# A planner counts eight transfers in flight on each queue: attention and a two-layer network on one core

## The chip, the cores and the metric

One core of a Trainium2 chip runs the whole program in one launch. The metric is the device time of one execution in microseconds (us), taken as the median over runs. TensorE (PE in the views) multiplies matrices, VectorE (DVE), ScalarE (ACT) and GpSimd (POOL) do element work, SyncE (SP) issues most transfers.

## The reference

```python
def _attn_ref(q, k, v, f):                     # (8, 8, 576, 64) each, f (8, 8, 576)
    scores = scale * np.matmul(q, k.transpose(0, 1, 3, 2))
    cum = np.cumsum(np.log(np.clip(f, 0.0001, 1.0)), axis=-1)
    scores = np.where(causal, -1000000000.0, scores + cum[:, :, :, None] - cum[:, :, None, :])
    attn = softmax(scores)                     # max taken off, sum + 1e-9
    return np.matmul(attn, v)

def _moe_ref(x, w_in, w_out, alpha):           # x (4608, 512), w_in (512, 2048)
    h = x @ w_in
    g = np.maximum(h, 0.0) + alpha * np.minimum(h, 0.0)
    return g @ w_out
```

The attention's output, with batch and position as rows and the 8 heads of 64 side by side, is the x of the two-layer network. All is 32-bit.

## The kernel before

**Attention.** The 64 heads are taken as 32 pairs, four pairs (0 to 3) for each of 8 batches; pair n belongs to batch n // 4. Pairs 0 to 8 transpose their exponentials on TensorE. Pairs 9 to 31 go through the function `turned`: TensorE makes the scores of both heads in one step of 24 matmuls (`run1`) and the last 64 query rows in a step of 6 (`run2`); VectorE adds the decay and takes the maximum (line 853, and 917 for the tail), ScalarE takes exponentials (line 833), VectorE turns 32x32 blocks (line 890), and sixteen transfers of 100 KB put the blocks in place (line 927, `big<-big`), eight of them issued by SyncE and eight by GpSimd. The product with v (`pv`, 60 matmuls) of pair n stands on TensorE behind `run1` of pair n + 2. ScalarE copies it out (966, 967), GpSimd scales it (989, 992), ScalarE rounds it (995) and GpSimd takes what the rounding left (996): rounded value and remainder together are a split x, one of four column groups of its batch.

**First layer.** For each batch there are 16 column blocks of h (`ffn1`, block 0 to 15). A block is two halves of six matmuls of 128x512 on one bank: the first half needs x of the batch's first two pairs, the second half x of its last two. ScalarE and VectorE evict a bank (1042, 1044) into one of three slots of a ring (`hs`, a part of `hx`), and a transfer of 256 KB stores the slot to DRAM (1046, `hd<-hx`). A slot is free again when its store has landed. The buffers of split x are six, of which a batch needs four; those of the first two column groups come free when the first half of block 15 is through. First-layer blocks of one batch fill TensorE beside the attention of the next two.

**Second layer.** From about 603 us the stored h comes back and is multiplied in 18 units; nothing of the attention is left by then.

**What sets the order.** Every step is an `op` with an engine, an estimated length, a key and its inputs. `Plan.run` plays the program through once while it is built: at each turn it looks over the steps whose inputs are planned, gives each the earliest start `s` that its engine, inputs and buffers allow, takes the smallest `(s, key)` on each engine and emits the earliest of these. Each engine runs its instructions in that order. A store of h has key -1000 and so goes first among steps that can start at the same time. A transfer (`kb` above 0) keeps its queue for its issue alone, some 0.4 us, and is planned to land after a common channel has moved it:

```python
if o.kb:
    self.chan = max(self.chan, s + 1.4) + o.kb / (220.0 if s < FAR else 280.0)
    end = self.chan + (0.0 if s < 4 else 2.0)
```

The built program has a rule of its own, which can be read in its waits: SyncE's transfers use eight channels (DMAHW0 to DMAHW7) in turn, and each waits until the one before it on its channel, the eighth ahead of it, has landed. It does so before the change and after it. The planner before does not know of it.

Of the kernel before, what the change touches and what calls it, by code (L numbers as in the profile page):

```python
# [53 lines left out]
class Store:  # L54


    def __init__(self, items):
        self.items, self.rings = items, []
        self.free = [(0.0, i) for i in range(len(items))]
# [30 lines left out]

SLACK = {"DVE": 1.12, "ACT": 1.08, "POOL": 1.05}
ENGS = ("PE", "ACT", "DVE", "POOL", "SP", "-")


class Plan:
    def __init__(self):
        self.now = dict.fromkeys(ENGS, 0.0)
        self.chan = 0.0
        self.ops = []
        self.banks = self.fill = None  # L100
        self.rnd = random.Random(SEED)
# [27 lines left out]
    def run(self):  # L129
        ops, self.ops = self.ops, []  # L130
        cand = {e: [] for e in ENGS}
        for o in ops:
            if o.n == 0:
                cand[o.eng].append(o)
        left = len(ops)
        mine = set(ops)
        while left:
            best = None
            for e in ENGS:
                t0 = self.now[e]  # L140
                pick = None
                for o in cand[e]:
                    r = o.ready
                    for b in o.bufs:
                        if b.t is not None:
                            continue
                        k = b.seq - b.ring.next
                        if k and not any(o2.ring is b.ring and o2.seq == b.ring.next for o2 in o.bufs):
                            r = None
                            break  # L150
                        a = b.ring.at(k)
                        if a is None:
                            r = None
                            break
                        if a > r:
                            r = a
                    if r is None:
                        continue
                    s = t0 if t0 > r else r
                    if pick is None or (s, o.key) < pick[:2]:  # L160
                        pick = (s, o.key, o)
                if pick is not None and (best is None or pick[0] < best[0]):
                    best = pick
            assert best is not None, "the plan is stuck"
            s, _, o = best
            self.t = s
            cand[o.eng].remove(o)
            left -= 1
            end = s + o.ns
            t0_, new = self.now[o.eng], []  # L170
            if o.two:
                end += max(0.0, self.now["POOL"] - s)
            self.now[o.eng] = end
            if o.kb:
                self.chan = max(self.chan, s + 1.4) + o.kb / (220.0 if s < FAR else 280.0)
                end = self.chan + (0.0 if s < 4 else 2.0)
            o.start, o.end = s, end
            for b in o.bufs:
                if b.t is not None:
                    continue  # L180
                st = b.ring.store
                f = min(st.free)
                st.free.remove(f)
                b.i, b.t = f[1], st.items[f[1]]
                if o.eng == "PE" and st is self.banks:
                    new.append((f[0], b.t))
                b.ring.next += 1
                b.ring.held += 1
            if new and self.fill and s < FILL:
                self.fill(new[0][1], s - max(t0_, new[0][0]))  # L190
            o.fn()
            for b in o.bufs:
                b.left -= 1
                b.last = max(b.last, end)
                if b.left == 0:
                    b.ring.held -= 1
                    b.ring.store.free.append((b.last + 0.3, b.i))
            for c in o.outs:
                c.n -= 1
                c.ready = max(c.ready, end + self.lag(o, c))  # L200
                if c.n == 0 and c in mine:
                    cand[c.eng].append(c)
# [1210 lines left out]
```

## Time and profile before

| | |
|---|---|
| median of 3 runs | 1011.52 us (1011.07 to 1012.36) |
| profiled execution | 1009.73 us, of which the span from first to last instruction is 1007.9 us |
| TensorE | busy 998.3 us (99%), mean granted clock 0.998 |
| VectorE, ScalarE, GpSimd | 815.2 us (81%), 592.7 us (59%), 394.4 us (39%) |
| transfers | 191.05 MB, 190 GB/s in the mean |

A group of matmuls in the timeline is given with its start and length; since matmuls are pipelined, the next group starts some 0.1 us before such a length is over. A wait in square brackets is idle time of the engine and what ended it. All matmuls stand on the helper's line 371, so they are told apart by what they read: `xx,wi` is the first layer, `Qhl` the scores, `big,vr` the product with v.

### The profile page before, as it was taken

The numbers are of one execution on the slowest core, as the hardware profiler recorded it, in microseconds if no ns is written. First come the engines' busy times: TensorE is split into PE (matmuls) and PEld (weight loads), VectorE is DVE, ScalarE is ACT, GpSimd is POOL, SyncE is SP. The second block draws the span as 40 slices with busy tenths as digits, with TensorE's granted clock in tenths as the row PEclk, the third lists the DMA queues.
The fourth block names the chain that finished last, engine by engine and source line by source line (L and its number), as shares of the span: only waits on it lengthen the run. The fifth ranks groups of instructions, "written<-read, shape, count | busy, mean of one in ns | idle before, by whom it ended". The sixth has DMA issues, their size and how long they took to land.

```text
span 1007.9 us, 21097 instructions
## 1 busy us (share of the span) xinstructions
PE 998.3 (99%) x7492; PEld 867.6 (86%) x7492; DVE 815.2 (81%) x1597; ACT 592.7 (59%) x1297; POOL 394.4 (39%) x635
## 2 busy tenths in 40 slices
PE   9999999999999999999999999999999999999998
PEld 6778888888878878888888888899999999999998
DVE  7878768888768838858754988699999999999994
ACT  7987876766657637656543766564553636444541
POOL 4575758799978857869650100000000000000000
PEclk9999999999999999999999999999999999999999
DMA  7988748989997987978867677543434344334421
GB/s 221 262 243 240 233 128 216 250 260 252 262 244 207 254 220 214 255 228 230 221 186 234 208 221 215 162 128 116 146 127 140 112 148 146 121 112 160 131 85 42
DMA packets 167545, 191.05 MB, mean 190 GB/s; under 512 B 22089, under 2 KB 116593, under 8 KB 167441
## 3 DMA queue, kind: packets, MB, share of 16 engines
q1 hardware_dynamic: 161264, 170.66, 57.8%
q0 software_dynamic: 5888, 18.85, 7.1%
q8 instruction: 59, 0.97, 0.4%
q14 instruction: 46, 0.37, 0.1%
q10 hardware_dynamic: 288, 0.20, 0.1%
HBM read 102.74 MB, written 48.80 MB: 150 GB/s over the span
## 4 chain that ended last, share of the span: by engine, by line
PE 88%; DMA 8%; SPq 2%; DVE 1%; issue 1%; ACT 0%; DVEq 0%; ACTq 0%
PE bank L371 84%; DMA big<-big 3%; PE bank L591 3%; DMA hd<-hx 2%; SPq L927 1%; DMA vr<-in_vv_dram 1%; DMA rqk<-in_qk_dram 1%; DVE big L890 0%; PE bank L439 0%; DMA Z<-c 0%; DVE hx L1044 0%; ACT hx L1042 0%; PE bank L473 0%; DMA rd<-st 0%; DVE Z L498 0%
## 5 line engine op out<-in xcount | busy, mean ns | idle before, releaser
L371 PE MATMUL bank<-xx,wi 128*128 128x512 f32 x1728 | 409.0, 393 | 0.3 <-POOL xx L996 0.3
L371 PEld LDWEIGHTS bank<-xx,wi 128*128 128x128 f32 x1728 | 320.3, 188 | 67.3 <-POOL xx L996 0.9
L371 PE MATMUL bank<-wi,gh 128*128 128x256 f32 (+1 forms) x1308 | 183.0, 301 | 0.0
L371 PE MATMUL bank<-wot,gh 128*128 128x256 f32 (+1 forms) x1308 | 183.0, 301 | 0.0
L371 PEld LDWEIGHTS bank<-wot,gh 128*128 128x128 f32 x1308 | 171.9, 191 | 9.6
L371 PEld LDWEIGHTS bank<-wi,gh 128*128 128x128 f32 x1308 | 171.8, 191 | 9.5
L833 ACT ACTIVATE big<-big,st 128x384 f32<-128x384 f32 (+4 forms) x207 | 118.6, 575 | 40.6 <-DVE st L853 40.5
L1044 DVE SCALAR_TENSOR_TENSOR hx<-bank,sa,hx 128x512 f32<-128x512 f32 x96 | 71.3, 744 | 82.8 <-ACT hx L1042 81.2
L1042 ACT ACTIVATE hx<-bank,ab 128x512 f32<-128x512 f32 x96 | 66.0, 688 | 94.8 <-PE bank L371 66.3
L890 DVE STREAM_TRANSPOSE big<-big 128x1408 f32<-128x1408 f32 (+2 forms) x69 | 86.6, 1274 | 20.7 <-DMA vr<-in_vv_dram 9.7
L371 PEld LDWEIGHTS bank<-big,vr 128*64 128x64 f32 x1884 | 89.2, 137 | 12.3 <-issue 3.2
L371 PE MATMUL bank<-big,vr 128*64 128x128 f32 (+2 forms) x1884 | 95.8, 260 | 2.1 <-DVE st L616 1.1
L545 POOL TENSOR_TENSOR Qhl<-rqk,Qhl 128x640 fp32r<-128x640 f32 (+1 forms) x56 | 83.4, 1497 | 31.8 <-ACT Qhl L544 29.3
L927 POOL DMA_DIRECT2D big<-big x184 | 92.1, 507 | 8.5 <-DVE big L890 4.8
L371 PE MATMUL bank<-Qhl 64*128 64x512 f32 (+6 forms) x840 | 93.4, 326 | 1.5 <-DVE hx L1044 1.5
L371 PEld LDWEIGHTS bank<-Qhl 64*128 64x128 f32 (+1 forms) x840 | 74.9, 186 | 17.5 <-issue 8.8
L517 POOL TENSOR_TENSOR Z<-Z,hx 128x384 f32<-128x384 f32 x60 | 54.8, 924 | 27.0 <-DMA Z<-c 17.2
L1290 ACT ACTIVATE gh<-hg 128x768 fp32r<-128x768 f32 x28 | 23.7, 848 | 65.4 <-issue 28.4
L1290 ACT ACTIVATE gh<-wx 128x768 fp32r<-128x768 f32 x28 | 23.7, 847 | 63.5 <-PE bank L371 28.4
L1293 DVE TENSOR_TENSOR gh<-hg,gh 128x1792 fp32r<-128x1792 f32 x28 | 56.5, 2017 | 1.6 <-ACT gh L1292 1.6
L1293 DVE TENSOR_TENSOR gh<-wx,gh 128x1792 fp32r<-128x1792 f32 x28 | 56.2, 2017 | 0.1
L996 POOL TENSOR_TENSOR xx<-hx,xx 128x512 fp32r<-128x512 f32 x32 | 41.9, 1317 | 27.6 <-ACT xx L995 27.1
(157 smaller groups left out, 1315.3 us busy)
## 6 DMA issues: line engine op xcount, KB each, us to landing
hd<-hx SPq DMA_DIRECT2D x144, 256.0 KB, 3.7
big<-big SPq DMA_DIRECT2D x184, 100.0 KB, 5.4
big<-big POOLq DMA_DIRECT2D x184, 100.0 KB, 5.2
rqk<-in_qk_dram SPq DMA_DIRECT2D x28, 608.0 KB, 4.9
hg<-hd SPq DMA_DIRECT2D x28, 512.0 KB, 4.9
wx<-hd SPq DMA_DIRECT2D x28, 512.0 KB, 4.2
vr<-in_vv_dram SPq DMA_DIRECT2D x32, 320.0 KB, 3.7
big<-in_w_in_dram SPq DMA_DIRECT2D x16, 512.0 KB, 5.2
```

Source lines behind the costliest of these rows:

```text
L371: pe.matmul(o, lhsT, rhs, start=start, stop=stop)
L517: m1 = op("POOL", c_po(128 * 3), lambda z4=z4: po.tensor_tensor(z4()[:, 6:9], z4()[:, 0:3], tb(3), ALU.add), kc + 0.1, got + [o_mask], [bZ])
L545: o2 = op("POOL", c_po(w), lambda hi=hi, lo=lo, raw=raw: po.tensor_tensor(lo(), raw(), hi().bitcast(F32), ALU.subtract), kc, [o1], [bqk, bQ])
L591: pe.transpose(t[:, c : c + 128], src[:, 128 * j : 128 * j + 128], ident)
L833: sums.append(op("ACT", c_exp(w), lambda: ac.activation(at(), at(), AF.Exp, bias=lo()[:, col : col + 1], scale=-1.0, accum_out=su()[:, col ...
L890: ve.transpose(t_t[:, :, c0 : c0 + 32 * (b1 - b0)].rearrange("p k (b c) -> p k b c", c=32), bE.t[:, 128 * off : 128 * (off + b1 - b0)].rea ...
L927: moves.append(op(n_, 550 if i % 2 else 450, lambda a=a, k=k, q_=q_: q_.dma_start(bM.t[32 * k : 32 * k + 32, a], t_t[32 * a : 32 * a + 32, ...
L996: xl = op("POOL", c_po(512), lambda: po.tensor_tensor(bx.t[:, 1], bxs.t[:, 0:512], bx.t[:, 0].bitcast(F32), ALU.subtract), st, [xh], [bxs, ...
L1042: cp = op("ACT", c_act(512), lambda bh=bh, bs=bs, fc=fc: ac.activation(bs.t, bh.t, AF.Relu, scale=ab[:, fc : fc + 1]), -1000, [last, o_sg] ...
L1044: cp = op("DVE", c_dve(512), lambda bh=bh, bs=bs, fc=fc: ve.scalar_tensor_tensor(bs.t, bh.t, sa[:, fc : fc + 1], bs.t, ALU.mult, ALU.add), ...
L1290: h0 = op("ACT", c_acs(3 * 128 * GW), lambda bhx=bhx, bgh=bgh: ac.activation(bgh.t[:, 0, 0:3], bhx.t[:, 1:4], AF.Copy), key, o1, [bhx, bgh])
L1293: his, rdy = [h0, h1], [op("DVE", c_tt(7 * 128 * GW), lambda bhx=bhx, bgh=bgh: ve.tensor_tensor(bgh.t[:, 1], bhx.t[:, 1:8], bgh.t[:, 0].bi ...
```

## The change

The planner keeps, for each queue, the planned landings of its transfers; a transfer is not planned to start before the landing of the eighth one ahead of it on its queue. No step, length, key or seed changes; the same instructions are emitted in another order.

```diff
+DEEP = 8
@@ class Plan, __init__
         self.chan = 0.0
+        self.flying = {e: [] for e in ENGS}
@@ run
                     s = t0 if t0 > r else r
+                    if o.kb and len(self.flying[e]) >= DEEP:
+                        s = max(s, self.flying[e][-DEEP])
                     if pick is None or (s, o.key) < pick[:2]:
@@
                 end = self.chan + (0.0 if s < 4 else 2.0)
+                self.flying[o.eng].append(end)
```

Lines of the kernel after are five higher (371 becomes 376). TensorE's order is the same up to where the trace has 79 us and again from the product with v of the last pair (535 us). Between them `run1` of pairs 10 to 18 stands behind 36 to 60 more first-layer matmuls than before, of pairs 19 to 22 behind 36 more, and of the pairs from 23 on at nearly the old place (24 fewer to 6 more).

TensorE before, at the passage from batch 1 to batch 2 of the first layer (`big,vr`: product with v of pair 12; each `xx,wi ... x6` is one half of a block, each `x12` a block):

```order
L371 MATMUL bank_83<-xx,wi 128x512 x6
L371 MATMUL bank_76<-big,vr_105 64x128 x20
L371 MATMUL bank_79<-big,vr_105 64x64 x10
L371 MATMUL bank_78<-Qhl_99 128x320 x3
L371 MATMUL bank_81<-Qhl_99 128x256 x3
L371 MATMUL bank_83<-xx,wi 128x512 x6
L371 MATMUL bank_80<-xx,wi 128x512 x12
L371 MATMUL bank_82<-xx,wi 128x512 x12
```

TensorE after, the same passage (`big,vr_106`: product with v of pair 11; then `run2` of pair 13, block 15 of batch 1, four first halves and, from `bank_78` on its second row, the second halves of batch 2):

```order
L376 MATMUL bank_78<-big,vr_106 64x128 x20
L376 MATMUL bank_82<-big,vr_106 64x64 x10
L376 MATMUL bank_80<-Qhl_100 128x320 x3
L376 MATMUL bank_79<-Qhl_100 128x256 x3
L376 MATMUL bank_83<-xx,wi 128x512 x12
L376 MATMUL bank_78<-xx,wi 128x512 x6
L376 MATMUL bank_81<-xx,wi 128x512 x6
L376 MATMUL bank_77<-xx,wi 128x512 x6
L376 MATMUL bank_76<-xx,wi 128x512 x6
L376 MATMUL bank_78<-xx,wi 128x512 x6
L376 MATMUL bank_81<-xx,wi 128x512 x6
L376 MATMUL bank_77<-xx,wi 128x512 x6
```

Before, the second half of block 0 of batch 2 follows its first half at once, and between pair 11's product with v and that second half stand the scores and the product with v of pair 12. After, pair 12 is behind the passage, and 39 first-layer matmuls stand between pair 11's product with v and the first matmul that reads pair 11's x.

SyncE before, the load of q and k (`rqk`) of pair 21, which stands right ahead of the eight moves (`big<-big`) of pair 17, with the channel that each transfer waits for:

```order
L491 DMA rqk_98<-in_qk_dram 128x2x608 [waits DMAHW1_49,Pool_49]
L927 DMA big<-big 32x800 [waits DMAHW2_49,DVE_49]
L927 DMA big<-big 32x800 [waits DMAHW3_49]
L927 DMA big<-big 32x800 [waits DMAHW4_49]
L927 DMA big<-big 32x800 [waits DMAHW5_49]
L927 DMA big<-big 32x800 [waits DMAHW6_49]
L927 DMA big<-big 32x800 [waits DMAHW7_49]
L927 DMA big<-big 32x800 [waits DMAHW0_49]
L927 DMA big<-big 32x800 [waits DMAHW1_49]
L821 DMA vr_105<-in_vv_dram 128x640 [waits DMAHW2_49,PE_49]
L1046 DMA hd<-hx 128x4x128 [waits DMAHW3_49,DVE_49]
L1046 DMA hd<-hx 128x4x128 [waits DMAHW4_49,DVE_49]
```

SyncE after, the load of the same pair's q and k:

```order
L496 DMA rqk_98<-in_qk_dram 128x2x608 [waits DMAHW3_49,Pool_49]
L1051 DMA hd<-hx 128x4x128 [waits DVE_49]
L932 DMA big<-big 32x800 [waits DMAHW5_49,DVE_49]
L932 DMA big<-big 32x800 [waits DMAHW6_49]
L932 DMA big<-big 32x800 [waits DMAHW7_49]
L932 DMA big<-big 32x800 [waits DMAHW0_49]
L932 DMA big<-big 32x800 [waits DMAHW1_49]
L932 DMA big<-big 32x800 [waits DMAHW2_49]
L932 DMA big<-big 32x800 [waits DMAHW3_49]
L932 DMA big<-big 32x800 [waits DMAHW4_49]
L943 DMA rd_64<-st_110 128x32 [waits DMAHW5_49,DVE_49]
L826 DMA vr_105<-in_vv_dram 128x640 [waits DMAHW6_49,PE_49]
```

Before, the last of the eight moves waits for the channel of the load (DMAHW1), and the two next stores of h stand behind it. After, the moves are those of the same pair 17, one store has come between load and moves, the next stands behind all twelve, and now the seventh move waits for the load's channel (DMAHW3 there).

## Rows read from the trace of the kernel before

**Rows 1.** The page, part 1: busy time, share and instructions of each engine.

```profile
PE 998.3 (99%) x7492; PEld 867.6 (86%) x7492; DVE 815.2 (81%) x1597; ACT 592.7 (59%) x1297; POOL 394.4 (39%) x635
```

**Rows 2.** Busy time of each engine in four stretches (header: the columns).

```profile
core 0: us, PE busy (x) PEld busy (x) DVE busy (x) ACT busy (x) POOL busy (x), PEclk, DMA share, GB/s
80.00:280.00 200.00, 200.00 (x1679) 165.87 (x1678) 160.59 (x397) 139.82 (x375) 158.99 (x239) 1.00 0.82 228
280.00:320.00 40.00, 38.49 (x287) 31.66 (x286) 28.15 (x70) 24.31 (x64) 30.76 (x50) 0.96 0.86 234
360.00:380.00 20.00, 18.73 (x146) 15.46 (x145) 8.06 (x20) 9.14 (x19) 9.94 (x15) 1.00 0.82 226
380.00:1000.00 620.00, 620.00 (x4345) 558.94 (x4344) 520.52 (x836) 329.08 (x589) 117.34 (x188) 1.00 0.55 164
```

**Rows 3.** TensorE in order of time, 294 to 306 us (start, length, what, idle before).

```profile
294.76 0.97 PE L371 MATMUL bank<-Qhl 64*128 64x512 f32 x6
296.06 0.44 PE L371 MATMUL bank<-Qhl 64*128 64x384 f32 x1 [0.34 <-DVE hx L1044]
297.68 1.49 PE L371 MATMUL bank<-Qhl 64*128 64x384 f32 x17 [1.17 <-DVE hx L1044]
299.09 2.88 PE L371 MATMUL bank<-xx,wi 128*128 128x512 f32 x6
301.90 3.30 PE L371 MATMUL bank<-big,vr 128*64 128x128 f32 x60
305.13 1.06 PE L371 MATMUL bank<-Qhl 128*128 128x320 f32 x6
```

**Rows 4.** The same view, 364 to 379 us.

```profile
363.81 5.18 PE L371 MATMUL bank<-xx,wi 128*128 128x512 f32 x22
369.27 3.45 PE L371 MATMUL bank<-xx,wi 128*128 128x512 f32 x14 [0.28 <-POOL xx L996]
372.65 2.19 PE L371 MATMUL bank<-Qhl 64*128 64x512 f32 x24
375.84 2.98 PE L371 MATMUL bank<-big,vr 128*64 128x128 f32 x60 [0.99 <-DVE hx L1044]
```

**Rows 5.** The same view, 218 to 235 us.

```profile
218.05 2.98 PE L371 MATMUL bank<-big,vr 128*64 128x128 f32 x60
220.97 1.06 PE L371 MATMUL bank<-Qhl 128*128 128x320 f32 x6
221.87 6.99 PE L371 MATMUL bank<-xx,wi 128*128 128x512 f32 x30
228.79 2.19 PE L371 MATMUL bank<-Qhl 64*128 64x512 f32 x24
232.50 2.99 PE L371 MATMUL bank<-big,vr 128*64 128x128 f32 x60
```

**Rows 6.** ScalarE in order of time, two evictions of the first layer.

```profile
294.54 0.69 ACT L1042 ACTIVATE hx<-bank,ab 128x512 f32<-128x512 f32 x1 [7.14 <-DMA hd<-hx]
...
360.09 0.69 ACT L1042 ACTIVATE hx<-bank,ab 128x512 f32<-128x512 f32 x1 [6.27 <-DMA hd<-hx]
```

**Rows 7.** SyncE in order of time: transfers as it issued them.

```profile
278.42 0.46 SPq L491 DMA_DIRECT2D rqk<-in_qk_dram  x1
278.97 10.05 SPq L927 DMA_DIRECT2D big<-big  x8
...
290.24 0.92 SPq L1046 DMA_DIRECT2D hd<-hx  x2
```

**Rows 8.** SyncE's waits from 250 to 380 us: total, times, longest.

```profile
SPq L927 <- DMA rqk<-in_qk_dram: 8.7, 3, 4.0
```

**Rows 9.** Line 491 (the q and k loads): issue to landing, all 28.

```profile
DMA to landing us min/median/max: 4.3/4.9/10.1
```

**Rows 10.** GpSimd in order of time: low parts of x.

```profile
230.75 1.28 POOL L996 TENSOR_TENSOR xx<-hx,xx 128x512 fp32r<-128x512 f32 x1 [0.18 <-ACT xx L995]
245.67 1.30 POOL L996 TENSOR_TENSOR xx<-hx,xx 128x512 fp32r<-128x512 f32 x1
...
366.68 2.54 POOL L996 TENSOR_TENSOR xx<-hx,xx 128x512 fp32r<-128x512 f32 x2 [2.14 <-ACT xx L995]
```

## The prediction

> **What bounds the kernel now.** I read the page's table of engines first. TensorE is busy for 99% of the span [rows 1], so an edit of the order can only win what TensorE loses: idle time, and time at a lower clock. The other four engines count only where TensorE waits for them. The table of stretches says where it loses. From 80 to 280 us and from 380 to 1000 us it is busy all the time, and the granted clock is 1.00 [rows 2]. Between them it falls short: 1.51 us of idle time from 280 to 320 us, at a mean clock of 0.96, and 1.27 us from 360 to 380 us at 1.00 [rows 2]. The order after is the old one up to about 79 us and again from 535 us on, so these places are all that it can win. (The start, before 79 us, is left as it is.)
>
> TensorE in order of time shows what each costs, three places in all.
>
> At 294.8 us `run1` of pair 19 waits 0.34 and 1.17 us for banks that ScalarE's side of the eviction frees late (the waits end on DVE, L1044). Then it runs slow: six 128x512 first-layer matmuls take 2.88 us, where 30 take 6.99 us [rows 3, 5]. Taken start to start, the 24 score matmuls, the six and the 60 of `pv` take 305.13 − 294.76 = 10.37 us [rows 3]. Clean, the same take 2.19 + 6 × 0.2307 + 2.92 = 6.49 us: 2.19 is the length of 24 score matmuls in one piece, 2.92 is 220.97 − 218.05, and 0.2307 is (228.79 − 221.87) / 30 [rows 5]. So **3.9 us** are lost. Of these 1.7 are the clock's: (301.90 − 299.09) − 1.38 = 1.43 on the six and (305.13 − 301.90) − 2.92 = 0.31 on the 60. The six run at half the speed of rows 5, that is at 1.2 GHz for 2.4.
>
> At 369.27 us the second halves of a batch wait for x: 36 matmuls take 372.65 − 363.81 = 8.84 us, clean 36 × 0.2307 = 8.30, so **0.5 us** [rows 4]. At 375.84 us a `pv` waits 0.99 us, and its 60 matmuls then take their usual 2.98 us: **1.0 us**, no lower clock [rows 4]. In sum 3.9 + 0.5 + 1.0 = 5.4 us.
>
> ScalarE's rows name the cause: evictions of the first layer at 294.54 and 360.09 us had waited 7.14 and 6.27 us for a store of h to land, since all three slots were taken [rows 6]. SyncE's rows say why the store was late. A load of q and k goes out at 278.42, the eight moves behind it take 10.05 us to issue, and the two stores behind them come only at 290.24 [rows 7]. The eighth move needs the load's channel, and the load lands late: issue to landing is 4.9 us in the median and 10.1 at most [rows 9]. SyncE's waits from 250 to 380 us have this in three places, 8.7 us in all [rows 8].
>
> **The change, part by part.** It adds and removes no instruction, so every term is a wait.
>
> *Stores ahead of moves.* SyncE's order after has a store between that load and the moves, and the load's channel is wanted by the seventh move. One slot of three is then free before the moves begin. The next store stands behind moves, decay rows and v, as before. ScalarE had to wait some 7 us for three slots; one early store lets it go on by one bank of twelve matmuls, 12 × 0.2307 = 2.8 us. In addition 36 to 60 more first-layer matmuls now stand ahead of `run1` of pairs 10 to 22, 36 × 0.2307 = 8.3 us: `run1` wants its banks and its q and k later than before, while the moves still end when they ended. 2.8 + 8.3 = 11.1 us is more than the 7.14 [rows 6], so I take the wait of `run1` as gone, with the 0.99 at `pv`, which has the same cause, and the 0.5 at the second halves, which now stand elsewhere. Bounds: nothing won at all (0), or all 5.4. I take **−5.4**, the nearer to the rows, as the needed slack is covered with 4 us to spare.
>
> *Loads of w_in for the last blocks* go out later, behind stores, from 80 to 150 us. TensorE has no idle time there now [rows 2], and its first-layer backlog hides them. With that cover gone it is a wait like the 0.99 of rows 4; as for a gain, there is no idle time to win. I take 0.
>
> *The new passage from batch 1 to batch 2.* Here the order takes a cover away. The second half of a block of batch 2 reads pair 11's x. Before, pair 12's scores and its `pv` stood between pair 11's `pv` and that half. After, `run2` and 39 first-layer matmuls do: 0.90 us (221.87 − 220.97) + 39 × 0.2307 = 9.9 us [rows 5]. The path of x from `pv` to the last low part can be read on the neighbours: `pv` of pair 12 ends at 218.05 + 2.98 = 221.03 and the low part at 230.75 + 1.28 = 232.03, so 11.0 us; pair 13's `pv` ends at 232.50 + 2.99 = 235.49, its low part at 245.67 + 1.30 = 246.97, so 11.5 us [rows 5, 10]. TensorE then waits 1.1 to 1.6 us; I take **+1.3**. Bounds: nothing, where GpSimd and ScalarE meet less work on that path; and 7.14 us, where ScalarE, which must copy and round on it, stands in a wait like that of rows 6. I take a value near the low end, since it comes from two rows of the same step. A gain is excluded, as no idle time stands there [rows 2].
>
> *Its clock.* An idle time of 0.34 + 1.17 us was followed by the half clock, one of 0.99 us was not [rows 3, 4]. 1.3 lies nearer to 1.51 (0.2 off) than to 0.99 (0.3 off), so I add the clock's **+1.7**; the bounds are 0 and 1.7.
>
> The sum is −5.4 + 1.3 + 1.7 = −2.4 us. The profiled execution took 1009.73 us, the median of the runs is 1011.52, which is 1.79 more; I take the difference over to after. So a profiled execution of 1007.3 and a median of **1009.1 us**.
>
> **The rivals.**
>
> *The new passage is hidden as well.* Then 1011.52 − 5.4 = 1006.1. For it: 1.3 us is little, and rows 10 show that GpSimd's step itself waits only 0.18 us, so a quieter ScalarE would shorten the path. Against it: both neighbours agree within 0.5 us.
>
> *The landing of the load sets the pace, not the order of issue*, so that the change doesn't do what it says. The 10.1 us of the load are about twice the median of its line [rows 9], and this load has sixteen moves beside it [rows 7]. If what the engines carry beside it makes it late, a store put between lands late too, its slot stays taken, and the loss of 294 us stays: only 0.5 + 1.0 are won, −1.5 + 3.0 = +1.5, so 1013.0. For it: DMA engines are busy for 0.86 of the time from 280 to 320 us [rows 2]. Against it: the stores lose their time before issue, at 290.24 [rows 7], and `run1` has more ahead of it. The Trainium skill, in "DMA: Bandwidth & Descriptors", section "Issuing engines are not separate DMA queues", says that transfers run interleaved on the same 16 DMA engines whoever issued them, and that spreading the issue saves only sequencer time; by that rule this rival would hold. The trace agrees as far as 10.1 us against 4.9 goes; that SyncE stood for 10.05 us over eight moves speaks for the queue as the place of the loss.
>
> *Slower: x is late at every passage.* The order after puts the second halves close behind `pv` not only at batch 2. At the two later passages about 24 matmuls and some scores stand between, some 6.2 us from the first half of block 15 on. The point at which it decides: the low part of a batch's last pair ends more than 6.2 us after that half begins. Before, this is seen once, at 369.27, where the two low parts from 366.68 on (2.54 us, having waited 2.14) held TensorE up [rows 4, 10]. Three passages at 1.3 + 1.7 = 3.0 make 9.0; less 5.4 that is +3.6, so 1015.1. For it: ScalarE and GpSimd are shared with evictions and moves, and more first-layer work now crowds there. Against it: that one wait was 0.28 us and came in the same disturbed stretch as the 6.27 us of rows 6, whose cause I expect gone.
>
> **How the numbers follow.** About 0.2%, 2.0 us, is what a measurement of this kernel can tell from no change: faster is below 1009.5, slower above 1013.5. My forecast, 1009.1, has a chance of 0.42; the two unknowns in it (1.1 to 1.6, the clock's 1.7) and small waits elsewhere make it 1007.4 to 1010.8. The hidden passage has 0.17, the landing rival 0.22, late x 0.19. Faster: all of the hidden passage, and somewhat over half of the forecast (0.27), together 0.44. Slower: late x whole, less a little, and the top of the landing rival (with the clock falling once more), 0.21. The same: 0.35. The range of 1006.0 to 1015.3 runs from the hidden passage to late x; what it leaves out is more wins than I count, at the bottom, and an added wait of 7.14 us, at the top.
>
> **What would show it.** Right, step by step: ScalarE's evictions (line 1047 after) without waits for `hd<-hx` of over 3 us between 280 and 380 us; no idle time ahead of `run1` of pair 19 nor of the `pv` behind it; TensorE's granted clock 1.00 from 280 to 320 us; one idle time of 1 to 2 us ended by GpSimd's low part (line 1001 after) at about 222 to 226 us, with first-layer matmuls at about half speed behind it. Without the idle time it is the hidden passage; with the same ScalarE waits after a load that takes 10 us, the landing rival; with idle times ended by line 1001 at three passages, late x. The forecast is wrong if TensorE waits for something else, q and k or decay rows above all, since their loads now stand behind more stores; or if the order between 79 and 535 us leaves TensorE without work where before it had none to spare.

## The result: slower, by loads that make the moves late

Six executions after the change took 1017.57 us in the median (1014.96 to 1020.23), six of the kernel before on the same chip 1011.3 (1009.39 to 1012.67): a ratio of **1.0063** (95% interval 1.0050 to 1.0077), 6.3 us slower. The forecast was 1009.1, its range ended at 1015.3.

The profiled execution after took 1020.23 us, the slowest of its six, and so is 10.5 us over the profiled 1009.73 of before. Its page has TensorE busy for 1.9 us more, in a span that is 10.6 us longer than that of [rows 1]:

```profile
PE 1000.2 (98%) x7492; PEld 871.7 (86%) x7492; DVE 814.2 (80%) x1597; ACT 593.3 (58%) x1297; POOL 393.7 (39%) x635
```

The busy time by stretches, to be held against [rows 2], shows where:

```profile
core 0: us, PE busy (x) PEld busy (x) DVE busy (x) ACT busy (x) POOL busy (x), PEclk, DMA share, GB/s
80.00:220.00 140.00, 140.00 (x1107) 116.44 (x1106) 107.06 (x266) 100.71 (x267) 97.25 (x140) 1.00 0.73 205
220.00:260.00 40.00, 35.55 (x275) 28.89 (x274) 26.11 (x63) 21.91 (x58) 27.39 (x45) 1.00 0.85 225
280.00:300.00 20.00, 17.95 (x138) 15.62 (x138) 15.88 (x43) 11.04 (x31) 16.95 (x31) 0.91 0.83 221
340.00:380.00 40.00, 35.40 (x267) 30.24 (x264) 29.36 (x68) 20.24 (x53) 29.34 (x45) 0.96 0.87 232
380.00:1000.00 620.00, 619.71 (x4365) 557.34 (x4364) 522.08 (x848) 332.83 (x598) 124.67 (x206) 1.00 0.57 170
```

TensorE is idle for 4.45, 2.05 and 4.60 us in three stretches, and in two of them its clock is down as well. The kernel before lost 2.8 us of idle time in all between 280 and 380 us. TensorE in order of time gives the places (start, length, what, idle before):

```profile
224.37 4.83 PE L376 MATMUL bank<-xx,wi 128*128 128x512 f32 x20 [0.89 <-POOL xx L1001]
229.13 1.79 PE L376 MATMUL bank<-Qhl 64*128 64x512 f32 x18
232.93 0.38 PE L376 MATMUL bank<-Qhl 64*128 64x256 f32 x1 [2.02 <-DVE hx L1049]
233.59 0.62 PE L376 MATMUL bank<-Qhl 64*128 64x256 f32 x5 [0.28 <-DVE hx L1049]
234.45 2.99 PE L376 MATMUL bank<-big,vr 128*64 128x128 f32 x60 [0.24 <-DMA xt<-hx]
237.36 1.06 PE L376 MATMUL bank<-Qhl 128*128 128x320 f32 x6
...
288.89 2.20 PE L376 MATMUL bank<-Qhl 64*128 64x512 f32 x24
293.14 4.64 PE L376 MATMUL bank<-big,vr 128*64 128x128 f32 x60 [2.06 <-DMA rd<-st]
297.71 1.07 PE L376 MATMUL bank<-Qhl 128*128 128x320 f32 x6
...
312.33 2.19 PE L376 MATMUL bank<-Qhl 64*128 64x512 f32 x24
314.46 2.99 PE L376 MATMUL bank<-big,vr 128*64 128x128 f32 x60
317.37 0.82 PE L376 MATMUL bank<-Qhl 128*128 128x320 f32 x4
...
353.56 2.19 PE L376 MATMUL bank<-Qhl 64*128 64x512 f32 x24
359.34 4.30 PE L376 MATMUL bank<-big,vr 128*64 128x128 f32 x60 [3.58 <-DMA rd<-st]
363.57 1.07 PE L376 MATMUL bank<-Qhl 128*128 128x320 f32 x6
```

At 312 us `run1` of pair 19 and the `pv` behind it are clean: 2.13 and 2.91 us from start to start. Those are the yardstick. `run1` of pair 14 and its `pv` take 237.36 − 229.13 = 8.23 instead of 5.04 us, so 3.2 are lost. At pair 16's `pv` it is 297.71 − 288.89 = 8.82, so 3.8; at pair 20's 363.57 − 353.56 = 10.01, so 5.0. The two `pv` behind the longest waits also ran slow, 4.6 and 4.2 us from start to start. With the 0.9 at 224 us and four losses between 0.3 and 1.2 us (at 243.8, 252.1, 345.2 and 523.2 us) that makes 16.3 us. Before it was 5.4; the difference, 10.9, is close to the 10.6 us by which the span of the profiled execution grew.

What a `pv` waits for must be read with care. The row names a transfer of decay rows (`rd`), but that is only what came last on the same channel; of all transfers, `pv` of this pair waits for its sixteen moves alone in the built program. SyncE's queue and GpSimd's at pair 20 show them:

```profile
343.99 0.47 SPq L496 DMA_DIRECT2D rqk<-in_qk_dram  x1
344.56 10.60 SPq L932 DMA_DIRECT2D big<-big  x8
356.79 0.34 SPq L943 DMA_DIRECT2D rd<-st  x1
```

```profile
343.82 1.54 POOL L932 DMA_DIRECT2D big<-big  x3 [1.76 <-DVE st L937]
345.57 2.45 POOL L932 DMA_DIRECT2D big<-big  x5 [0.20 <-issue]
```

GpSimd issues its eight moves in some 4 us. SyncE takes 10.60 us for its eight, since the eighth wants the channel of the load of pair 24, issued at 343.99 and landed, by the trace, at 354.6. The last move landed at 358.5, and the `pv` started at 359.34. It is the queue of [rows 7] again, and worse. The loads now land later:

```profile
DMA to landing us min/median/max: 5.2/7.9/10.6
```

This view, and that of [rows 9], must be read with care too: it counts only the loads whose landing the profile tells, 4 of 28 here and 14 of 28 before, not all 28. A load has landed by the last rise of its channel's count ahead of the next transfer on that channel. Followed so, all 28 took 5.0 us in the median before and 6.5 after, 10.7 and 11.6 at most.

The other end of the same thing, at 232.93 us: SyncE issued the eight moves of pair 12 in 10.72 us, from 216.28 on, behind another load and a store of h that took 10.4 and 10.9 us to land, and the next store of h went out at 227.12. ScalarE's eviction waited for it, and `run1` of pair 14 for the bank:

```profile
230.70 0.69 ACT L1047 ACTIVATE hx<-bank,ab 128x512 f32<-128x512 f32 x1 [3.50 <-DMA hd<-hx]
```

### The profile page after: what moved, and what is told of

It is laid out like the page before. It is cut to its first block, busy times and chain, and to the rows that moved or that the text cites. A ratio compares the mean times of both kernels' runs of the same rounds, so it can differ in the third digit from the quotient of the medians.

```text
span 1018.5 us, 21107 instructions
## 1 busy us (share of the span) xinstructions
PE 1000.2 (98%) x7492; PEld 871.7 (86%) x7492; DVE 814.2 (80%) x1597; ACT 593.3 (58%) x1297; POOL 393.7 (39%) x635
## 4 chain that ended last, share of the span: by engine, by line
PE 90%; DMA 4%; DVE 2%; SPq 2%; ACT 1%; issue 1%; DVEq 0%; ACTq 0%
PE bank L376 87%; PE bank L596 2%; DMA big<-big 1%; DMA vr<-in_vv_dram 1%; SPq L932 1%; DMA rd<-st 1%; PE bank L444 1%; DMA xt<-hx 0%; DVE big L895 0%; DMA hd<-hx 0%; DVE hx L1049 0%; DVE big L858 0%; DVE Z L503 0%; PE bank L478 0%; DVE Zt L505 0%
## 5 line engine op out<-in xcount | busy, mean ns | idle before, releaser
L376 PE MATMUL bank<-big,vr 128*64 128x128 f32 (+2 forms) x1884 | 98.5, 264 | 7.4 <-DMA rd<-st 5.6
L376 PEld LDWEIGHTS bank<-big,vr 128*64 128x64 f32 x1884 | 92.0, 140 | 15.3 <-issue 8.7
L1295 ACT ACTIVATE gh<-hg 128x768 fp32r<-128x768 f32 x28 | 23.7, 848 | 65.6 <-PE bank L376 28.5
L1044 ACT ACTIVATE hx<-bank,sg 128x512 f32<-128x512 f32 x48 | 32.9, 688 | 35.4 <-PE bank L376 21.6
```

What stands on the lines that cost most here:

```text
L376: pe.matmul(o, lhsT, rhs, start=start, stop=stop)
L1044: cp = op("ACT", c_act(512), lambda bh=bh, bs=bs, fc=fc: ac.activation(bs.t, bh.t, AF.Copy, scale=sg[:, fc : fc + 1]), -1000, [last, o_sg] ...
L1295: h0 = op("ACT", c_acs(3 * 128 * GW), lambda bhx=bhx, bgh=bgh: ac.activation(bgh.t[:, 0, 0:3], bhx.t[:, 1:4], AF.Copy), key, o1, [bhx, bgh])
```

## The experiments

**Theory (the queue):** a load of q and k that stands right ahead of a pair's moves on SyncE lands late; the moves behind it wait on its channel; `pv`, the turns and the stores wait for the moves. **Rivals:** the new order is too tight by itself; the moves are slow because the DMA engines are shared, whatever stands where; or orders simply scatter, and this one came out badly.

### Taking the loads out of the moves' way

The order of every engine but SyncE stays word for word. A table holds a load back while the program is emitted, until the eight moves are out:

```diff
+HOLD = {124: 108.05, 134: 118.05, 144: 128.05, 154: 138.05, 184: 168.05, ...}
@@ run
-            o.fn()
+            if o.kb == 608 and o.key in HOLD:
+                self.kept[HOLD[o.key]] = o.fn
+            else:
+                o.fn()
+            if o.eng == "SP" and o.key in HOLD.values():
+                self.seen[o.key] = self.seen.get(o.key, 0) + 1
+                if self.seen[o.key] == 8:
+                    self.kept.pop(o.key)()
```

> The change, with nine loads of q and k (of pairs 14 to 17, 20, 21, 24, 25, 29) emitted behind the eight SyncE moves that they stand ahead of; every other engine's order is that of the change, word for word. Queue theory (the moves wait on the channel of a load that takes about 10 us, land late, and hold up the product with v, the turns and the stores): SyncE's moves issue in about 7 us instead of 9 to 11, the waits of TensorE at 232.9, 293.1 and 359.3 us and the half clock behind them go, 1006.5 to 1010.5 us. Tight-order theory (the new order leaves two blocks less one half between a pair's scores and its product with v, and pulls pair 12 behind the passage; that alone is too little): at least half of the loss stays, 1013.5 to 1017.5. Bandwidth theory (moves are slow because the DMA engines are shared): moves still take 9 to 11 us, within 1 us of 1017.5.

> The kernel before, with six loads of q and k (of pairs 16, 17, 20, 21, 24, 25) emitted behind the SyncE moves that they stand ahead of; nothing else moves. Queue theory: the wait ahead of run1 of pair 19 with its half clock (3.9 us) and the 0.99 us at 375.8 go, 1005.5 to 1008. Tight-order theory: the same or less, 1006 to 1010. Bandwidth theory: within 1 us of 1011.3.

Measured: the change with nine loads held **1006.9 us** (ratio to before 0.9963, 0.9949 to 0.9976), the kernel before with six held **1006.13** (0.9955, 0.9940 to 0.9969). The change's profile now has at pair 20 the whole thing undisturbed. SyncE:

```profile
335.21 7.39 SPq L943 DMA_DIRECT2D big<-big  x8
342.70 1.07 SPq L507 DMA_DIRECT2D rqk<-in_qk_dram  x1
```

TensorE, `run1` of pair 22 and the `pv` of pair 20, with no idle time:

```profile
344.62 2.19 PE L387 MATMUL bank<-Qhl 64*128 64x512 f32 x24
346.74 2.98 PE L387 MATMUL bank<-big,vr 128*64 128x128 f32 x60
349.66 1.06 PE L387 MATMUL bank<-Qhl 128*128 128x320 f32 x6
```

The five loads whose landing this view tells took 4.8 us in the median, 6.5 at most; by channel all 28 took 4.9 and at most 7.7:

```profile
DMA to landing us min/median/max: 4.3/4.8/6.5
```

Over the pairs whose moves start between 190 and 385 us, SyncE's eight take 8.2 us in the mean (9.8 in the change, 9.0 before), not quite the 7 expected. So 10.7 us went by putting nine loads in other places, and the tight-order theory, which kept half of the loss, falls for this order; so does the one on shared engines as it stood, by which the moves are slow whatever stands where, since the same bytes move. The 0.89 us at the new passage went too: TensorE has no wait for the low part there.

By which road the load holds up the moves is not separated by these runs. A load held back neither blocks a channel of SyncE nor moves its data beside the moves, and no run takes away one of the two alone. The trace of the change shows both at pair 20. GpSimd issued its eight moves in 4.2 us, with no wait for SyncE's channels, and the last of them still landed only at 356.89 us; they took 6.3 to 9.4 us to land, with the loads held 5.3 to 6.3. TensorE was ready for this `pv` at 355.76. So without SyncE's queue `pv` would still have waited, by an estimate from these times, for 1 to 2 of its 3.58 us. SyncE's queue made the rest, and the late store at 227.12 us, whose data were ready at 218.65.

### Which of the loads

> The change, with only those six loads behind the moves that stand ahead of moves in the kernel before as well (of pairs 16, 17, 20, 21, 24, 25). If the change costs more because the same loads meet an order with less room: 1007 to 1010, nearly as good as with all nine. If it costs more because it puts further loads (of pairs 14, 15, 29) ahead of moves: 1012 to 1016.

> The change, with only those three loads behind the moves that only the change puts ahead of moves (of pairs 14, 15, 29). Less room: 1015 to 1018, no gain. Further loads: 1010 to 1013.

Measured: with the six loads that stand ahead of moves in both kernels held, 1008.18 us (0.9970, 0.9956 to 0.9983); with the three that only the change puts there, 1015.51 (1.0045, 1.0031 to 1.0058). The six carry 9.4 us of the change's loss; the three carry about 2, which is not clear of the two intervals. In the kernel before the same six carry 1011 − 1006.1 = 4.9 us. So the change costs more mostly at the same loads.

### Is it the rule, or one order of many?

The rule first: built for SyncE's queue alone it gives the change's order on every engine, and built for GpSimd's alone, or with twelve in place of eight, that of before. So only SyncE's floor of eight changes anything. Then its time, and the seed:

```diff
-                    if o.kb and len(self.flying[e]) >= DEEP:
+                    if o.kb and s < 100 and len(self.flying[e]) >= DEEP:
```

```diff
-SEED = 66
+SEED = 67
```

> The rule holds only up to 100 us of the plan; from there on the planner chooses as it did before. If the rule's choices from 100 us on make the loss: 1009 to 1013. If the first choices do, by setting an order that then runs on by itself (ten loads of q and k stand ahead of moves in it, up to pair 24): 1014 to 1020.

> The change with the planner's random seed 67 instead of 66, which shakes the estimated lengths by up to 3%. If the loss belongs to the rule: 1016 to 1020, 5 to 8 us over the kernel before with the same seed. If it belongs to the one order that came out: anything from 1006 to 1018, no nearer to 1017.6 than to 1011.3.

> The kernel before with seed 67. If the loss belongs to the rule: 1009 to 1014. If orders scatter whatever the rule: up to 6 us from 1011.3 to either side.

Measured: rule up to 100 us only, 1018.08 us (1.0083, 1.0056 to 1.0110); seed 67 with the rule 1019.09 (1.0096, 1.0074 to 1.0118), without it 1016.11 (1.0050, 1.0032 to 1.0069). A few choices before 100 us set another order, and that order runs on by itself. And a shake of the estimates by 3% moves the kernel before by 5 us, almost as much as the change does; the rule costs 6.3 us at one seed and 3.0 at the other, where 5 to 8 were expected if the loss belonged to the rule. In the profiled execution of before with seed 67 (1020.83 us, the slowest of nine) SyncE's moves wait for loads seven times between 140 and 400 us, 18.0 us in all (8.7 in three at seed 66). The change with seed 67 fits less well: there it is 4.5 us in three, and the largest single wait of TensorE past 79 us is for a low part at the new passage:

```profile
227.97 4.80 PE L376 MATMUL bank<-xx,wi 128*128 128x512 f32 x20 [2.68 <-POOL xx L1001]
```

That asks for a test of the theory on orders that nobody arranged by hand.

### A rule for the loads

```diff
+        self.gone = {}
@@ run
                     r = o.ready
+                    if o.kb == 608 and o.key >= 114 and self.gone.get(o.key // 10 - 2, 0) < 8:
+                        continue
@@
             o.fn()
+            if o.eng == "SP" and o.kb == 100:
+                self.gone[o.key // 10] = self.gone.get(o.key // 10, 0) + 1
```

> The kernel before, with one more rule in the planner in place of a table: the load of q and k of a pair may not start before the eight SyncE moves of the pair four earlier have been issued. The order is another one from about 150 us on. Queue theory: 1005 to 1008.5, as with the six loads put back by hand. If orders scatter for other reasons: anything from 1006 to 1018.

> The change, with the same rule for the loads. Queue theory: 1005 to 1008.5, within 2 us of the kernel before with that rule, so that the change itself is worth nothing either way once the loads are out of the moves' way. If the change has a cost of its own: 1011 or more.

> The kernel before with seed 67 and the rule for the loads; without it, seed 67 took 1016.1 us. Queue theory: 1005 to 1009. If the scatter of the orders has another source: 1012 to 1018.

> The change with seed 67 (1019.1 us, the slowest order of the four) and the rule for the loads. Queue theory: 1005 to 1009. If the change has a cost of its own at this seed: 1012 or more.

| | seed 66 | seed 67 |
|---|---|---|
| before | 1011.3 | 1016.11 |
| before, rule for the loads | **1004.75** (0.9947, 0.9928 to 0.9967) | 1005.23 (0.9948, 0.9931 to 0.9964) |
| the change | 1017.57 | 1019.09 |
| the change, rule for the loads | 1005.92 (0.9954, 0.9936 to 0.9971) | 1012.83 (1.0018, 1.0008 to 1.0028) |

(Intervals: against the kernel before at seed 66 on the same chip.) Every order gains, some 6 to 12 us, and three of four come out within 1.2 us of each other, faster than both kernels. So the place of the loads counts in orders that the planner found by itself, too. The fourth misses its range by 4 us and falls into that of the other reading, a cost of the change's own at this seed: a further loss of some 7 us is not the loads'. Its TensorE has, among others,

```profile
226.13 4.82 PE L381 MATMUL bank<-xx,wi 128*128 128x512 f32 x20 [1.06 <-POOL xx L1006]
...
351.89 2.98 PE L381 MATMUL bank<-big,vr 128*64 128x128 f32 x60 [1.92 <-DMA rqk<-in_qk_dram]
```

so the new passage costs 1.06 us in this order, and one `pv` waits for moves of which SyncE issued the last at 345.1 and which landed at 351.0, with no load issued among them. What makes them late was not tried.

### Why the same loads cost the change more: two tries, not settled

First idea: *room*. Between the scores of pair n + 2 and the `pv` of pair n the kernel before keeps a half block for the nine pairs 9 to 17, the change keeps none. Its `pv` of pair 16 starts 30.4 us after its `run1` ended, of which nothing is a wait; in the change it is 30.5 us, of which 2.06 are. The moves needed 30.2 and 29.9 us. At pair 20 it is the other way round: neither order has a half block there, TensorE was ready for `pv` 28.5 us after `run1` before and 29.7 after, and the moves needed 28.2 and 32.4. So by the traces pair 16 lost its time to less room and pair 20 to slower moves. To test room I moved `pv` behind the next block in the change, and took the half block out of the kernel before.

```diff
+LATER = (180.01, 220.01)
@@ run
-            o.fn()
+            slots = {(id(b.ring.store), b.i) for b in o.bufs}
+            if o.eng == "PE" and o.key in LATER:
+                self.kept, self.more = [(o, slots)], 2
+            elif any(o in x.outs or slots & y for x, y in self.kept):
+                self.kept.append((o, slots))
+            else:
...
```

> The change, with the products with v of pairs 16 and 20 moved on TensorE behind run2 and one half block that follow them (0.9 + 1.4 = 2.3 us more room for the moves); the loads stay ahead of the moves. Less-room theory: the wait of 2.06 us and its half clock (1.7) at pair 16 go, of the 3.58 us at pair 20 about 1.3 stay and its half clock goes (1.3), so about 7 us less, 1009 to 1012.5. If room does not matter (the lateness only moves on to the next wait): 1015 to 1018.

> The change, with the products with v of pairs 16 and 20 (and run2 of pairs 18 and 22, which shares a bank with them) moved on TensorE behind the next block of twelve first-layer matmuls, 2.8 us more room; the loads stay ahead of the moves. One load of v goes out four moves later, nothing else moves. Room theory: the waits of 2.06 and 3.58 us and the half clocks behind them (1.7 and 1.3) nearly go, 1009 to 1012. If room does not matter, since the lateness moves on to the next wait: 1015 to 1018.

Measured: 1032.04 and 1024.22 us (1.0129, 1.0109 to 1.0149, for the second). In the first, users of the same buffers were not held back along with the two products, which waited 9.7 us for moves of a later pair and multiplied that pair's data; it tells nothing. In the second the arithmetic is whole, but the block put ahead has no bank: it waits for VectorE to empty the scores, 4.92 us at pair 16 and 4.74 at pair 20, more than the wait it was to fill:

```profile
294.64 5.49 PE L391 MATMUL bank<-xx,wi 128*128 128x512 f32 x12 [4.92 <-DVE st L873]
```

The other way round, nine half blocks of the kernel before go behind `pv`:

```diff
+TIGHT = (110, 120, 130, 140, 150, 160, 170, 180, 190)
@@ emit
+        if o.eng == "PE" and self.pv and not self.kept and o.key != self.pv:
+            self.kept = [(o, slots)]
...
```

> The kernel before, with the half block that stands between the scores of pair n + 2 and the product with v of pair n moved behind that product, for the nine pairs 9 to 17; every other engine's order is that of before. This is the change's order at these places: 1.4 us less room for the moves. Room theory (late moves cost only where the product with v stands right behind them): pairs 12, 13 and 16, which had 1.4, 0.7 and 0.3 us to spare, now wait up to 1.1 us each, some with the half clock behind: 1012.5 to 1017. If room is nothing: within 1 us of 1010.7.

> The same nine half blocks moved, with the six loads behind the moves (which alone took 1006.1 us). Room theory: the moves land in time, so the lost half costs nothing, 1005.5 to 1008. If the moved half blocks have a price of their own (banks, evictions): the same loss as between b_tight and before, 1009 or more.

Measured: 1016.4 us (1.0055, 1.0034 to 1.0075), and with the loads held 1013.34 (1.0023, 1.0008 to 1.0038). The first falls into the range of the room theory, the second does not: the moved half blocks cost 7.2 us with the loads held too (1006.13 to 1013.34). The places tell more than the times. With the loads ahead of the moves, `pv` waits at three of the nine pairs, 12, 13 and 16, those that had least to spare:

```profile
221.64 2.99 PE L390 MATMUL bank<-big,vr 128*64 128x128 f32 x60 [1.56 <-DMA hd<-hx]
238.83 4.56 PE L390 MATMUL bank<-big,vr 128*64 128x128 f32 x60 [2.87 <-DMA hx<-rd]
284.14 2.99 PE L390 MATMUL bank<-big,vr 128*64 128x128 f32 x60 [0.92 <-DMA big<-big]
```

With the loads held the waits at 12 and 16 are gone: there the half block had covered late moves. Three dear places are in the trace of both runs (here with the loads held):

```profile
178.23 1.07 PE L401 MATMUL bank<-Qhl 128*128 128x320 f32 x6 [1.56 <-DVE hx L1074]
194.32 1.07 PE L401 MATMUL bank<-Qhl 128*128 128x320 f32 x6 [1.56 <-DVE hx L1074]
238.01 4.65 PE L401 MATMUL bank<-big,vr 128*64 128x128 f32 x60 [3.81 <-DMA hx<-rd]
```

Two are a price of the moved half itself: `run2`, right behind it now, waits for its eviction, 3.1 us in all. The third is late moves once more, by another road (again the name in the row is only a neighbour on the channel). GpSimd's eight moves stood behind two low parts of x that had waited for ScalarE:

```profile
224.56 2.54 POOL L1026 TENSOR_TENSOR xx<-hx,xx 128x512 fp32r<-128x512 f32 x2 [2.46 <-ACT xx L1025]
227.04 3.98 POOL L957 DMA_DIRECT2D big<-big  x8
```

SyncE's eight were out by then, and the held load started at 227.4, into the middle of GpSimd's. From the second on those landed 6 to 7 us after issue, the last at 237.2, and the `pv`, without its half block, stood waiting. So at this place the held load did harm, since GpSimd's moves were not out yet. But it is the smaller part: without the hold the same moves, issued from 228.80 on with no load issued among them, landed 4.0 to 5.7 us after issue, and `pv` still waited 2.87 us. Since the edit brought waits of its own, its time does not tell how much of the change's extra loss is room. Nor does the lack of the half block cost anything when the moves are prompt: the two fastest orders, with the rule for the loads on the kernel before, have `pv` right behind `run1` at 17 and 18 of the 20 pairs from 9 to 28, at 1004.75 and 1005.23 us, and the change with nine loads held has it at all 20, at 1006.9.

Second idea: *how far the load starts ahead of GpSimd's moves*. The load of pair 24 stands behind the same kinds of transfers in both kernels. Before, SyncE issued it at 327.99 us and GpSimd its moves from 328.76 on; the load landed in 7.5 us and SyncE's moves took 7.49:

```profile
327.99 0.64 SPq L491 DMA_DIRECT2D rqk<-in_qk_dram  x1
328.72 7.49 SPq L927 DMA_DIRECT2D big<-big  x8
```

```profile
328.76 3.98 POOL L927 DMA_DIRECT2D big<-big  x8
```

After, GpSimd was 0.17 us ahead (343.82 against 343.99), the load took 10.6 and the moves 10.60. One run starts the loads of pairs 20 and 24 two places earlier in the change:

```diff
+LEAD = (267, 336)
@@ run
+            if i + 1 in LEAD or i + 2 in LEAD:
+                self.back.append(o.fn)
...
```

> The change, with the loads of q and k of pairs 20 and 24 issued two places earlier on SyncE's queue, ahead of a transfer of x and a store of h, some 1 us sooner; they still stand ahead of the moves and all other orders are the change's. Lead theory (a load is slow if GpSimd's moves start before it or with it): the two loads land in 7 to 8.5 us instead of 10.2 and 10.6, the moves behind them issue in about 8 us, the waits of 2.06 and 3.58 us shrink to under 1 and under 2 us, 1010 to 1014. If any load near sixteen moves is as slow: 1016 to 1019.

Measured: 1015.72 us (1.0049, 1.0032 to 1.0066). That is 1.9 under the change, not clear of the two intervals, and in neither expected range. At pair 24's load it went as expected: 1.70 us ahead of GpSimd it lands in 7.9, the moves issue in 8.57, and the wait of `pv` falls from 3.58 to 1.41 us without a lower clock. At pair 20's, 1.0 us ahead, the load still took 9.6, the moves 10.40, and the wait 1.89:

```profile
276.82 0.38 SPq L509 DMA_DIRECT2D rqk<-in_qk_dram  x1
...
279.13 10.40 SPq L945 DMA_DIRECT2D big<-big  x8
...
342.68 0.58 SPq L509 DMA_DIRECT2D rqk<-in_qk_dram  x1
...
345.70 8.57 SPq L945 DMA_DIRECT2D big<-big  x8
```

```profile
291.68 2.99 PE L389 MATMUL bank<-big,vr 128*64 128x128 f32 x60 [1.89 <-DMA rd<-st]
...
357.73 2.98 PE L389 MATMUL bank<-big,vr 128*64 128x128 f32 x60 [1.41 <-DMA rd<-st]
```

So the lead made the difference at one place of two. Over the traces of all 18 kernels it counts, but not sharply: loads 1.3 to 2.5 us ahead of GpSimd's first move landed in 4.2 to 8.7 us, those 0.75 to 1.3 us ahead in anything from 4.9 to 11.5. How the extra loss divides between less room and slower loads **stays open** beyond the reading of pairs 16 and 20 above; that the same six loads cost 4.9 us in one order and 9.4 in the other is shown.

## Why the prediction was wrong, point by point

**The bound** was right: only TensorE's losses between 79 and 540 us moved.

**The step that failed is the term of −5.4**, "I take the wait of `run1` as gone", with its two supports. The old places are indeed clean (312.33 us), but the cause stayed and made losses of 3.2, 3.8 and 5.0 us elsewhere. First support: "`run1` wants its banks and its q and k later than before, while the moves still end when they ended". They don't. A pair's moves hang on its own `run1`, so they moved along: `run1` of pair 17 starts 17.0 us later than before (274.67 for 257.69), and SyncE issues the pair's last move 17.4 us later (305.9 for 288.5). The 8.3 us of slack never were. Second support: one store now goes ahead of the moves. It does, and ScalarE's waits for stores between 280 and 380 us fell from 21.5 us in seven to 7.7 in three (total, times, longest, before and after); but stores were only one of the things that the late moves hold up.

```profile
ACT hx L1042 <- DMA hd<-hx: 21.5, 7, 7.1
ACT hx L1047 <- DMA hd<-hx: 7.7, 3, 3.3
```

Of the prediction's signs of being right, the clean `run1` of pair 19 came; a clock of 1.00 from 280 to 320 us (0.91 up to 300) and no wait of ScalarE over 3 us (3.3) did not. Its sign of being wrong came: TensorE waits for something else, though for moves, not for q and k or decay rows.

**What I did not look at** was `pv` against the landing of its moves. In the trace of before the last move of pair 16 lands at 275.6 and its `pv` starts at 275.9, at pairs 13 and 20 it is 0.7 and 0.3 us. TensorE showed no wait there, so I took it as settled; it was the next wait in line. At pair 16 a `pv` due 2 us sooner after its `run1` was enough, at pair 20 a load that landed 3 us later. The prediction's 4.9 and 10.1 us for the loads rest on the 14 that [rows 9] counts; all 28 give 5.0 and 10.7, which changes none of its sums.

**The new passage** was right in place and mechanism and too large: 0.89 us at 224.37, ended by GpSimd's low part, for 1.3. Of the excess 0.23 is a count: 39 matmuls stand ahead of the first that reads pair 11's x, but 40 ahead of the first that reads its low part. The 20 matmuls behind it take 229.13 − 224.37 = 4.76 us, clean 20 × 0.2307 = 4.61: no half clock, so the +1.7 was wrong. Part of the wait was the loads' too, since with the loads held it is gone.

**The w_in loads** at nothing: right, TensorE has no idle time from 80 to 220 us.

**The rivals.** That landings set the pace was the right mechanism with the wrong price. I let it keep what was lost before (1013.0) and did not ask what a late landing would stop in another order. The Trainium skill, "DMA: Bandwidth & Descriptors", section "Issuing engines are not separate DMA queues", has the other half of it: transfers share the 16 DMA engines whoever issues them. The trace agrees: SyncE's load of pair 24 lands in 10.6 us beside GpSimd's moves and in 4.8 when it is held until both engines' moves are out. Late x at every passage, my slower case, came near in time (1015.1) by chance and was not what happened: only one passage shows a wait, of 0.89 us.

The rule itself does what it says. But it counts eight in flight with landings that the planner prices at about 6 us for a load, where such a load took 10; and a planner that knows that the queue is full still puts the load first, since it picks what can start earliest. Keeping the load back is what helped, with the count of eight or without it.

## What to carry to other kernels

On a queue in which each transfer waits for the one eight places ahead, a large transfer right ahead of a batch that somebody waits for delays the batch (here by some 3 us of issue at pair 20, 10.60 for 7.39): put it behind the batch, if its data are wanted much later (here the nine held loads were first read 7.5 us or more after landing). When a change moves an order, list for each engine not only the waits that exist but the ones that are missed by less than a microsecond, and read what else hangs on the transfer that is late. And before a rule of a planner is judged by one order, shake its estimates: here a seed was worth 5 us, and of the two rules the one that took the cause away gained in all four orders.

## What the runs showed of the hardware

- Landings of the 608 KB loads of before and after, followed by channel: with at most eight moves of 100 KB issued from 1 us ahead of the load until it landed, 38 loads took 3.9 to 8.1 us, 36 of them 7.0 or less; with thirteen or more, 16 loads took 6.1 to 11.6 us. In the traces of all 18 kernels 36 loads went out within 0.5 us of the first of a pair's sixteen moves; they took 7.1 to 11.6 us, 18 of them 9.6 or more.
- The length of an idle time alone did not tell what the clock does. After 2.06 us and 3.58 us the next 60 matmuls took 4.6 and 4.2 us for 2.9, at a granted clock of 0.91 in the mean of that 20 us stretch for the first; after 1.89 us, in the run with the earlier loads, and after 2.02, 0.28 and 0.24 us in a row at pair 14, they took 2.99 us, the full speed; before the change 0.34 and 1.17 us were followed by half speed [rows 3].
- Executions of one kernel spread unequally: the change by 5.3 us (six executions), the change with the earlier loads by 8.2 (twelve), before with the rule for the loads by 4.3 at seed 66 and by 1.3 at seed 67 (six each). No run shows what sets the spread.
